# Early branches through later code, prefetch hints at its end, and another first load, in a decode kernel fed by DMA

## Chip, cores, metric

One core of a Trainium2 chip. The metric is device time in microseconds (us) of one execution. All executions told of here were in the normal (fast) state.

## The reference

One decode step: layer norm of x, attention of 32 query heads over a cache of 65,536 positions in 4 key-value heads, and beside it a mixer MLP on the same normalized x. Both are added to x.

```python
# cut to what matters; shapes: D 1024, Hq 32, Hkv 4, Sk 65536, Dh 128, F 3584; bfloat16
xn  = layernorm(x)                                        # x: [1, 1, 1024]
q   = xn @ wq                                             # wq: [1024, 4096]
p   = softmax(q . k_cache * Dh**-0.5)                     # k_cache: [1, 4, 65536, 128]
a   = (p . v_cache) @ wo                                  # wo: [4096, 1024]
h   = gelu(layernorm(xn) @ w1)                            # w1, w2: [1024, 1024]
x1  = xn + shift(h) @ w2                                  # one token: the shifts leave zeros
b   = x1 + gelu(layernorm(x1) @ w3) @ w4                  # w3: [1024, 3584], w4: [3584, 1024]
out = x + a + b
```

170 MB are read, nearly all of it the cache, for one token.

## The kernel before

The parts that the change and the argument touch. Each engine's instructions are recorded in a queue (`q_pe`, `q_dve`, ...) and emitted at the end. All large loads go through SyncE's DMA queue (`q_sp`) into three slots of 8.4 MB; x goes through ScalarE's.

```python
        _dma(q_act, chan("x"), lambda e: e.dma_start(out=x_bf, in_=...), writes=[b_x])
        kv_load(0, "s0", rows_src(A_wq, 0, 8), 8 * HQD)          # 8.4 MB, 65,536 bytes a partition
        b_w1 = b_KV[1][0:2]
        b_w2 = b_KV[1][2:4]
        kv_load(1, "w1", rows_src(B_w1, 0, 8), 8 * D, b_w1)      # 2.1 MB, 16,384 bytes a partition
        _dma(q_sp, chan("w2"), ...)
        kv_load(2, "s2", rows_src(B_w3, 0, 8), 8 * F)
# ... cut: constants on POOL, layer norm, q projection, MLP; then for each of 8 blocks of the cache:
            Ttr(n)          # VectorE transposes K in place
            QK(n)           # TensorE: scores
            # ... cut: MAX, EXP, PT, PTr, PV, FLUSH
            issue(6 + 2 * m)                                     # V of the next block
            issue(7 + 2 * m)                                     # K of the one after
# ... cut; at the end w4 comes in four parts, each followed by its matmuls, then the output:
        for i, (r0, nr) in enumerate(w4_parts):                  # rows 17, 7, 3, 1
            out_rows([...], [b_W4[i], b_gh], last=(i == len(w4_parts) - 1))
        _op(q_dve, lambda e: e.tensor_copy(orow[:, :], OUT), reads=[b_OUT], writes=[b_orow])
        ev_out = _dma(q_sp, chan("out"), lambda e: e.dma_start(out=..., in_=orow[0:97:32, :]), reads=[b_orow])
        q_sp.wait_all([ev_out])
# emission: one straight program an engine; only TensorE has a loop, over the 4 heads
        for eng in (nc.sync.engine, nc.scalar.engine):           # one DMA of each goes ahead of the opening barrier
            first = next(i for i in code[n_before:] if i.engine == eng)
            code.remove(first)
            code.insert(code.index(heads[eng]), first)
        q_pool.emit(nc.gpsimd)
        q_dve.emit(nc.vector)
# ... cut
        q_pe.emit(nc.tensor, q_pe.ops[:marks[0]])
        with nc.tensor.Fori(0, HKV):
            # ... cut
        q_pe.emit(nc.tensor, q_pe.ops[marks[-1]:])
```

## Time and profile before

| | before |
|---|---|
| time | 400.48 us median of 3 runs (400.39 to 400.56) |
| span of the profile | 399.1 us |
| data moved | 169.87 MB, 426 GB/s |
| TensorE, VectorE busy | 42%, 55% |
| first matmul, q projection starts | 6.63, 27.53 us |
| last part of w4 landed: first engine, last engine | 394.45, 396.56 us |
| from there to the end of the span | 2.52 us |

The kernel keeps the 16 DMA engines full from the first microsecond to the last. Lines of the page of the kernel before: the DMA row (busy share in tenths in 40 slices of 10 us), and the queues (packets, MB, share of 16 engines' span). q1 is SyncE's data queue, q10 ScalarE's, and the two of kind "instruction" carry the engines' own code. In all lines of the profile PE is TensorE's matmuls, PEld its weight loads, DVE VectorE, ACT ScalarE, POOL GpSimd, SPq SyncE's queue, and L379 a line of the kernel; "engine" alone, in the text on packets, is one of the 16 DMA engines.

```profile
span 399.1 us, 3429 instructions
PE 168.9 (42%) x1523; PEld 59.0 (15%) x1484; DVE 221.4 (55%) x260; ACT 23.9 (6%) x50; POOL 7.7 (2%) x31
...
DMA  9999899999999999999999999999999999999995
...
q1 hardware_dynamic: 3608, 169.87, 98.7%
q8 instruction: 5, 0.08, 0.1%
q10 hardware_dynamic: 144, 0.00, 0.0%
q14 instruction: 2, 0.02, 0.0%
```

So the time is a sum of three: when the DMA engine that is done first has delivered its share of the last load, how much later the slowest engine is, and what follows. The compute is hidden. The next lines are from the chain that ended last (start, length, what): long DMA waits with short computations between them, and at the end a wait for w4, four matmuls and one copy.

```profile
0.12 22.10 DMA KV<-in_A_x_dram
...
27.53 5.03 PE S_ps L379 x64
...
138.97 46.66 DMA KV<-in_A_k_cache_dram
...
363.64 32.91 DMA KV<-in_B_w_dram
396.60 0.31 PE S_ps L566 x4
396.94 0.42 DVE orow L647
```

And from the waits of SyncE's queue (who waited for what: us, times, longest): the final wait, for the output to land.

```profile
SPq L73 <- DMA out_dram<-orow: 1.0, 1, 1.0
SPq L728 <- PEq L728: 0.3, 1, 0.3
```

The second line is the opening barrier.

The trace also records single packets. The table gives the instruction packets of the kernel before that ran within its span (start in us, duration, bytes, queue). Those on q8 are TensorE's; those on q14 are taken for VectorE's:

```
46.00  1.09 us  16384   q8        52.71  0.33 us  8192   q14
81.76  1.03     16384   q8       259.38  0.33     8192   q14
122.72 1.02     16384   q8
378.24 1.07     16384   q8
394.28 1.08     16384   q8
```

A 16,384-byte one and the data packet behind it, which takes 2.97 instead of 2.42 us, cost one engine about 1.6 us; a VectorE one 0.33 us and 0.66 us for its neighbour (3.08 us). The split of the data over the engines is static, as far as the trace shows: what an engine lost it did not make up. With the packets of each engine chained end to start, the engine that carried the fetch of 81.76 us was 1.72 us behind the first engine at 204 us and 1.71 us behind at 389 us. No packet of TensorE came between 122.72 and 378.24 us, while its loop ran three whole passes; the one in 147 to 225 us is 274 matmuls and 278 weight loads.

### The profile page before, as it was taken

The numbers are of one execution on the slowest core, as the hardware profiler recorded it, in microseconds if no ns is written. First come the engines' busy times: TensorE is split into PE (matmuls) and PEld (weight loads), VectorE is DVE, ScalarE is ACT, GpSimd is POOL, SyncE is SP. The second block draws the span as 40 slices with busy tenths as digits, with TensorE's granted clock in tenths as the row PEclk, the third lists the DMA queues.
The fourth block names the chain that finished last, engine by engine and source line by source line (L and its number), as shares of the span: only waits on it lengthen the run. The fifth ranks groups of instructions, "written<-read, shape, count | busy, mean of one in ns | idle before, by whom it ended". The sixth has DMA issues, their size and how long they took to land.

```text
span 399.1 us, 3429 instructions
## 1 busy us (share of the span) xinstructions
PE 168.9 (42%) x1523; PEld 59.0 (15%) x1484; DVE 221.4 (55%) x260; ACT 23.9 (6%) x50; POOL 7.7 (2%) x31
## 2 busy tenths in 40 slices
PE   0034767338033713460357036413541362137394
PEld 0011334012001210110012001101120110012232
DVE  0024222994298549833984597269647952895201
ACT  1000000011001100110011002000100110011000
POOL 5000000000000000000000000000000000000000
PEclk9998568555655665575557555855585558555969
DMA  9999899999999999999999999999999999999995
GB/s 420 420 388 493 383 441 466 447 415 427 420 427 429 434 460 434 434 427 420 434 427 420 466 440 434 421 420 434 427 427 466 434 440 420 420 427 434 418 414 229
DMA packets 3759, 169.97 MB, mean 426 GB/s; under 512 B 548, under 2 KB 552, under 8 KB 808
## 3 DMA queue, kind: packets, MB, share of 16 engines
q1 hardware_dynamic: 3608, 169.87, 98.7%
q8 instruction: 5, 0.08, 0.1%
q10 hardware_dynamic: 144, 0.00, 0.0%
q14 instruction: 2, 0.02, 0.0%
HBM read 169.87 MB, written 0.00 MB: 426 GB/s over the span
## 4 chain that ended last, share of the span: by engine, by line
DMA 59%; DVE 25%; PE 12%; issue 1%; ACT 1%; SPq 1%; POOL 0%
DMA KV<-in_A_k_cache_dram 45%; DVE KV L460 18%; DMA KV<-in_B_w_dram 8%; DMA KV<-in_A_x_dram 6%; PE S_ps L411 3%; PE OT_ps L518 2%; DVE mrow L481 2%; PE M_ps L426 2%; PE S_ps L474 2%; PE S_ps L379 1%; ACT p_sb L496 1%; DVE Yall L395 1%; DVE pT_f L509 1%; DVE pT_f L419 1%; PE PT_ps L505 0%
## 5 line engine op out<-in xcount | busy, mean ns | idle before, releaser
L460 DVE STREAM_TRANSPOSE KV<-KV 128x4096 f32<-128x4096 f32 x32 | 140.3, 4422 | 44.3 <-DMA KV<-in_A_k_cache_dram 44.3
L474 PE MATMUL S_ps<-KV,Ycur 128*32 128x512 bf16 x512 | 60.7, 624 | 132.5 <-DVE KV L460 132.5
L518 PE MATMUL OT_ps<-KV,pT_f 128*32 128x512 bf16 x512 | 47.2, 511 | 4.0 <-issue 3.0
L474 PEld LDWEIGHTS S_ps<-KV,Ycur 128*32 128x32 bf16 x512 | 14.3, 126 | 160.0 <-DVE KV L460 142.4
L496 ACT ACTIVATE p_sb<-S_ps,brun 128x1024 bf16<-128x1024 f32 x16 | 17.8, 1114 | 276.6 <-DVE brun L494 176.1
L509 DVE STREAM_TRANSPOSE pT_f<-PT_ps 128x512 f32<-128x512 f32 x32 | 22.5, 702 | 14.0 <-PE PT_ps L505 14.0
L481 DVE TENSOR_REDUCE mrow<-S_ps 128x1 f32<-128x1024 f32 x16 | 19.3, 1205 | 11.3 <-PE S_ps L474 11.3
L484 PE MATMUL M_ps<-Rm,Lmat 128*128 128x16 bf16 x16 | 3.1, 194 | 38.0 <-DVE Rm L482 38.0
L529 DVE SCALAR_TENSOR_TENSOR O_acc<-O_acc,ff,OT_ps 128x512 f32<-128x512 f32 x12 | 9.0, 748 | 14.7 <-PE OT_ps L518 14.7
L518 PEld LDWEIGHTS OT_ps<-KV,pT_f 128*32 128x32 bf16 x512 | 13.1, 115 | 23.8 <-issue 16.4
L411 PE MATMUL S_ps<-KV 128*32 128x512 bf16 x88 | 12.1, 538 | 2.7 <-DVE KV L359 2.7
L339 DVE CAST KV<-KV 128x8 f32<-128x8 bf16 x1 | 0.2, 172 | 22.2 <-DMA KV<-in_A_x_dram 22.2
L578 PE MATMUL S_ps<-KV,o_bf 128*1 128x512 bf16 x64 | 9.9, 484 | 4.5 <-DMA KV<-in_A_wo_dram 4.5
L505 PE MATMUL PT_ps<-p_sb,permR 128*128 128x512 bf16 x16 | 9.7, 607 | 0.8
L426 PE MATMUL M_ps<-ident_f,pT_f 64*128 64x2 f32 (+2 forms) x32 | 7.9, 373 | 2.5 <-DVE pT_f L419 2.5
L484 PEld LDWEIGHTS M_ps<-Rm,Lmat 128*128 128x128 bf16 x16 | 1.7, 104 | 49.3 <-DVE Rm L482 49.3
L582 DVE COPY pT_f<-S_ps 1x512 f32<-1x512 f32 x1 | 0.7, 679 | 14.4 <-PE S_ps L578 14.4
L426 PEld LDWEIGHTS M_ps<-ident_f,pT_f 64*128 64x128 f32 (+2 forms) x32 | 7.7, 326 | 4.7 <-DVE pT_f L419 3.1
L419 DVE COPY pT_f<-S_ps 64x512 f32<-64x512 f32 (+1 forms) x3 | 2.1, 685 | 10.8 <-PE S_ps L411 10.8
L505 PEld LDWEIGHTS PT_ps<-p_sb,permR 128*128 128x128 bf16 x32 | 3.3, 102 | 27.5 <-ACT p_sb L496 14.7
L364 PE MATMUL M_ps<-KV 8*128 8x8 bf16 x1 | 0.2, 184 | 16.1 <-DVE Dmat_f L363 16.1
L642 POOL MEMSET pT_f<- 64x512 f32 x1 | 0.5, 520 | 312.4 <-PE OT_ps L518 312.4
(88 smaller groups left out, 90.2 us busy)
## 6 DMA issues: line engine op xcount, KB each, us to landing
KV<-in_B_w_dram SPq DMA_DIRECT2D x1, 7168.0 KB, 48.0
KV<-in_B_w_dram SPq DMA_DIRECT2D x1, 4352.0 KB, 27.4
KV<-in_B_w_dram SPq DMA_DIRECT2D x2, 2048.0 KB, 28.3
KV<-in_B_w_dram SPq DMA_DIRECT2D x1, 1792.0 KB, 31.3
KV<-in_B_w_dram SPq DMA_DIRECT2D x1, 768.0 KB, 32.7
KV<-in_B_w_dram SPq DMA_DIRECT2D x1, 256.0 KB, 32.9
KV<-in_A_k_cache_dram SPq DMA_DIRECT2D x8, 46.7
KV<-in_A_v_cache_dram SPq DMA_DIRECT2D x8, 28.1
```

What stands on the lines that cost most here:

```text
L411: fns.append(lambda e, j=j, k=k, mv=mv: e.matmul(S_ps[32 * (k % 4):32 * (k % 4) + 32, bank + k // 4, :], vec[:, j:j + 1].broadcast_to([P, ...
L419: _op(q_dve, lambda e, b=b, nb=nb: e.tensor_copy(pT_f[0:32 * nb, b, :], S_ps[0:32 * nb, bank + b, :]), reads=[b_S[bank + b]], writes=[b_pT ...
L426: fns.append(lambda e, b=b, nb=nb, c=c: e.matmul(M_ps[:, c0 + 16 * b + c:c0 + 16 * b + 4 * nb:4], pT_f[0:32 * nb, b, c:512:4], ident_f[0:3 ...
L460: _op(q_dve, lambda e: e.transpose(out=KV32[:, s, o:o + 4096], in_=KV32[:, s, o:o + 4096]), reads=[b_KV[s][sub]], writes=[b_KV[s][sub]], l ...
L474: fns.append(lambda e, we=we, cm=cm, mv=mv: e.matmul(S_ps[32 * cm:32 * cm + 32, n % 4, :], Ycur[:, we, :, :].rearrange("p a g -> p (a g)") ...
L481: _op(q_dve, lambda e: e.reduce_max(mrow[:, k:k + 1], S_ps[:, 2 * k:2 * k + 2, :].rearrange("p b c -> p (b c)"), axis=AX.X), reads=b_S[2 * ...
L496: _op(q_act, lambda e: e.activation(p_sb[:, :, :].rearrange("p b c -> p (b c)"), S_ps[:, 2 * k:2 * k + 2, :].rearrange("p b c -> p (b c)") ...
L505: _op(q_pe, lambda e: e.matmul(PT_ps[:, :], permR[:, :], p_sb[:, n % 2, :], start=True, stop=True), reads=[b_p[n % 2], b_const], writes=[b ...
L509: _op(q_dve, lambda e: e.transpose(out=pT_f[:, n % 2, :], in_=PT_ps[:, :]), reads=[b_PT], writes=[b_pT[n % 2]], loop=True)
L518: fns.append(lambda e, q=q, q4=q4: e.matmul(OT_ps[32 * q4:32 * q4 + 32, g % 2, :], pT_bf[:, n % 2, q, :, 1], KV[:, s, 8192 * sub + 512 * q ...
L529: _op(q_dve, lambda e: e.scalar_tensor_tensor(out=O_acc[:, 0:512], in0=O_acc[:, 0:512], scalar=ff[:, k:k + 1], in1=OT_ps[:, k, :], op0=ALU ...
L578: _grp(q_pe, [lambda e, j=j, jj=jj: e.matmul(S_ps[32 * jj:32 * jj + 1, 1, :], o_bf[:, j:j + 1], KV[:, 0, j * D + 512 * jj:j * D + 512 * (j ...
```

## The change

Its intent: fetch code early instead of among the data. TensorE and VectorE jump through small stubs that lie further on in their code, so that instruction packets come at the start. The last part of the code of each has a hint (BRANCH_PREFETCH_HINT in the trace) that names a stub; it is meant to keep the packets of 259.38 and 394.28 us out of the data. w1 goes first because its packets are small (16,384 bytes in 0.61 us, against 65,536 in 2.42 for wq), so that early fetches and x, which share the engines with it, wait less. SyncE issues four loads ahead of the opening barrier instead of one.

```diff
@@ loads
-        kv_load(0, "s0", rows_src(A_wq, 0, 8), 8 * HQD)
         kv_load(1, "w1", rows_src(B_w1, 0, 8), 8 * D, b_w1)
+        kv_load(0, "s0", rows_src(A_wq, 0, 8), 8 * HQD)
@@ emission (cut)
-        for eng in (nc.sync.engine, nc.scalar.engine):
+        for eng, n_early in ((nc.sync.engine, 4), (nc.scalar.engine, 1)):
@@
-        q_dve.emit(nc.vector)
+        def visit(e, stub, nxt, back, within=None):
+            go(e, back)                       # branch over the stub
+            label(stub)
+            nc.engines[e].nop(nofuse=True)
+            go(e, nxt)                        # the early path goes on from here
+            label(back, within)
+
+        go(dve, "dve_v1")                     # first thing that VectorE does
+        label("dve_open")
+        open_barrier(dve)
+        q_dve.emit(nc.vector, q_dve.ops[:dve_cut])
+        visit(dve, "dve_v1", "dve_open", "dve_a")
+        go(dve, "dve_b")
+        label("dve_last")
+        nc.vector.nop(nofuse=True)
+        go(dve, "dve_end")
+        label("dve_b")
+        dve_hint = nc.vector.mark_branch_hint_location()
+        q_dve.emit(nc.vector, q_dve.ops[dve_cut:])
+        nc.vector.br("dve_last").branch_hint(dve_hint)
+        label("dve_end")
@@ TensorE (cut): stubs v1 and v2 ahead of the barrier, v3 and v4 after it, v2 and v3 inside the loop's body
+        go(pe, "pe_v1")
+        label("pe_open")
+        open_barrier(pe)
+        go(pe, "pe_v3")
+        label("pe_a")
...
+        label("pe_f")
+        pe_hint = nc.tensor.mark_branch_hint_location()
+        q_pe.emit(nc.tensor, q_pe.ops[pe_cut3:])
+        nc.tensor.br("pe_last").branch_hint(pe_hint)
+        label("pe_end")
```

The last branch of each engine goes back to a stub, and from there on to the end of the program.

More of the change, by code (lines that the diff above doesn't have):

```diff
@@ L447, in bass_parallel_sum__gqa_block_cached__mixer_s_mlp__decode_kernel @@
         layer_norm(x1, b_x1, xn3, xn3_bf, b_xn3, 208)
+        pe_cut0 = len(q_pe.ops)
         proj(2, 0, F, xn3_bf, 0, b_KV[2] + [b_xn3], 288)
@@ L639, in bass_parallel_sum__gqa_block_cached__mixer_s_mlp__decode_kernel @@
                 combine(h)
+            if m == 1:
+                dve_cut = len(q_dve.ops)
         loop_sync(HKV)
@@ L644, in bass_parallel_sum__gqa_block_cached__mixer_s_mlp__decode_kernel @@
         wo_rows()
+        pe_cut3 = len(q_pe.ops)
         for i, (r0, nr) in enumerate(w4_parts):
@@ L651, in bass_parallel_sum__gqa_block_cached__mixer_s_mlp__decode_kernel @@
         code = nc.m.functions[0].blocks[0].instructions
-        heads = {e: next(i for i in code if i.opcode == "Drain" and i.engine == e) for e in (nc.sync.engine, nc.scalar.engine)}
+        pe, dve = nc.tensor.engine, nc.vector.engine
+        opening = {e: [i for i in code if i.engine == e and i.opcode in ("Drain", "EventSemaphore")] for e in (pe, dve, nc.sync.engine, nc.scalar.engine)}
         n_before = len(code)
@@ L655, in bass_parallel_sum__gqa_block_cached__mixer_s_mlp__decode_kernel, with go, label, open_barrier @@
         q_act.emit(nc.scalar)
-        for eng in (nc.sync.engine, nc.scalar.engine):
-            first = next(i for i in code[n_before:] if i.engine == eng)
-            assert first.opcode == "DMACopy" and not first.sync_info.on_wait
-            code.remove(first)
-            code.insert(code.index(heads[eng]), first)
-        q_pool.emit(nc.gpsimd)
-        q_dve.emit(nc.vector)
+        for eng, n_early in ((nc.sync.engine, 4), (nc.scalar.engine, 1)):
+            for first in [i for i in code[n_before:] if i.engine == eng][:n_early]:
+                assert first.opcode == "DMACopy" and not first.sync_info.on_wait
+                code.remove(first)
+                code.insert(code.index(opening[eng][0]), first)
+        q_pool.emit(nc.gpsimd)
+        def go(e, name):
+            nc.br(name, engines=[e])
+        def label(name, within=None):
+            nc.switch_bb(name, parent=within)
+        def open_barrier(e):
+            here = nc.m.functions[0].blocks[-1].instructions
+            for i in opening[e]:
+                code.remove(i)
+                here.append(i)
+        def visit(e, stub, nxt, back, within=None):
[18 more added lines that the diff above has]
+        label("dve_end")
         marks = [i for i, o in enumerate(q_pe.ops) if o[0] == 3]
@@ L690, in bass_parallel_sum__gqa_block_cached__mixer_s_mlp__decode_kernel @@
             assert [(o[0], o[2]) for o in body] == [(o[0], o[2]) for o in work[0]]
-        q_pe.emit(nc.tensor, q_pe.ops[:marks[0]])
+        nc.tensor.nop(nofuse=True)
+        go(pe, "pe_v1")
+        label("pe_open")
+        n_pe = len(nc.m.functions[0].blocks) - 1
+        open_barrier(pe)
+        go(pe, "pe_v3")
+        label("pe_a")
+        q_pe.emit(nc.tensor, q_pe.ops[:pe_cut0])
+        visit(pe, "pe_v1", "pe_v2", "pe_b")
+        q_pe.emit(nc.tensor, q_pe.ops[pe_cut0:marks[0]])
         for s_, v in entry.items():
@@ L694, in bass_parallel_sum__gqa_block_cached__mixer_s_mlp__decode_kernel @@
         with nc.tensor.Fori(0, HKV):
-            for waits, o in zip(steps, work[0]):
+            body_bb = nc.bb_map[nc.m.functions[0].blocks[-1].name]
+            for k, (waits, o) in enumerate(zip(steps, work[0])):
+                if k == 100:
+                    visit(pe, "pe_v2", "pe_open", "pe_c", body_bb)
+                if k == 220:
+                    visit(pe, "pe_v3", "pe_v4", "pe_d", body_bb)
                 for s_, v in waits.items():
@@ L700, in bass_parallel_sum__gqa_block_cached__mixer_s_mlp__decode_kernel @@
                 nc.tensor.wait_ge(s_, v).then_inc(s_, -v)
-        q_pe.emit(nc.tensor, q_pe.ops[marks[-1]:])
+        q_pe.emit(nc.tensor, q_pe.ops[marks[-1]:pe_cut3])
+        visit(pe, "pe_v4", "pe_a", "pe_e")
+        go(pe, "pe_f")
+        label("pe_last")
+        nc.tensor.nop(nofuse=True)
+        go(pe, "pe_end")
+        label("pe_f")
[3 more added lines that the diff above has]
+        label("pe_end")
         prev, n_ld = None, 0
+        code = next(b for b in nc.m.functions[0].blocks if b.name == "pe_a").instructions
         for k, i in enumerate(code):
@@ L713, in bass_parallel_sum__gqa_block_cached__mixer_s_mlp__decode_kernel @@
             prev = key
-        assert n_ld > 40, n_ld
+        assert n_ld > 20, n_ld
 _INS = ['A_x', 'A_k_cache', 'A_v_cache', 'A_wq', 'A_wo', 'B_x', 'B_w1', 'B_w2', 'B_w3', 'B_w4']
```

## The prediction

> **What bounds the kernel.** The page has VectorE busy 55% and TensorE 42%; its queue part gives the data queue 98.7% of 16 engines' span: 169.87 MB, mean 426 GB/s. In the packet records a 65,536-byte packet takes 2.42 us, 27.07 bytes/ns an engine. An engine's 10.62 MB need 392.2 us; the first packet starts 1.0 us into the span, the first round of packets takes about 3.1 instead of 2.42 us, and what follows the last landing (396.56) takes 2.5 us. The table of DMA issues shows K loads waiting 46.7 us from issue to landing, although 8.39 MB at this rate take 19.4: queued work hides compute.
>
> **Where 2 us are left.** The packet records also hold instruction packets, placed among the data: five of 16,384 bytes (TensorE, at 46.0, 81.8, 122.7, 378.2, 394.3 us) and two of 8,192 (VectorE, 52.7 and 259.4). Each sits on one engine. A 16 KB one takes 1.03-1.09 us and the data packet beside it about 0.55 us more: 1.6 us. An 8 KB one takes 0.33 us and its neighbour 0.66 more: 1.0 us. Data are divided statically, so an engine never makes this up. Chaining packets end to start shows ten engines that finish at 394.0-394.6, five at about 395.4-396.0, and the one with both VectorE packets last, at 396.1. The final load therefore lands at 396.56, its first engine at 394.45: 2.1 us of skew, which is the whole prize.
>
> [...]
>
> **What the change does.** Branches through stubs pull TensorE's and VectorE's later blocks at the start[...]. w1 ahead of wq puts 16 KB packets (0.61 us) beside the early fetches and lets x, whose 16-byte packets alternate with the load in front, land near 6 us, not 22.2. [...] wq and w1 together still land near 26.9; the q projection starts near 27.3 (27.5 before). The first layer norm (5.3 us) fits long before that. Branches in the loop cost well under 1 us and are hidden.
>
> **On the critical path.** Only the slowest engine. Two fetches vanish, the rest move early but still occupy engines, save what runs before the first data packet at 1.0 us. No engine should carry two, so the slowest has +0.6 to +1.6 instead of +2.0: gain 0.4 to 1.4 us, at most 2.0. Prediction **399.5 us**, 8 in 10 between **398.3 and 400.6**; faster by over 2%: 0.01, within 2%: 0.98, slower by over 2%: 0.01.
>
> **Marks of each step.** Right: no 16,384-byte instruction packet after about 20 us; x lands at 5-8 us; w4's last landing 395-396.2, skew between its first and last engine 0.8-1.7 us; loop spacing (77.5 us for two blocks) and the tail of 2.5 us unchanged; DMA share 99%.
>
> **What would make it wrong.** Early fetches falling on one engine, adding up to more than 2 us;[...] the barrier so late that the q projection and with it the first K load slip past the queued 20 MB (beyond 47 us); a tail block missing at the end, a visible stall before the last matmuls; or early fetches that cost nothing, giving 398.4.

The sum: the slowest engine at +0.6 to +1.6 us instead of +2.0, so 0.4 to 1.4 us off 400.48, put at 399.5. But its "two fetches" that vanish (TensorE's of 394.3 us and VectorE's of 259.4) were then expectation only. Where the text has no figure, the traces have: a branch of TensorE's loop takes 0.08 to 0.23 us in the kernel before and 0.08 to 0.22 in the changed one, and x's 128 packets of 16 bytes come 16 to a round of data packets, each within 0.03 us of the end of one (both kernels). That a branch can stall is shown by the changed kernel (5.57 to 7.09 us).

## The result, and the profile after

| | before | changed |
|---|---|---|
| time | 400.44 us (400.37 to 400.56, 4 runs) | 400.87 us (400.77 to 401.15, 4 runs) |
| first matmul, q projection starts | 6.63, 27.53 us | 21.41, 28.49 us |
| x landed, wq landed | 22.21, 22.02 us | 11.32, 28.35 us |
| w4 landed: first engine, last engine | 394.45, 396.56 us | 394.52, 396.40 us |
| from there to the end | 2.52 us | 3.35 us |
| span | 399.1 us | 399.8 us |

The ratio is 1.0012 (95% interval 0.9994 to 1.0029). A ratio is the mean time of one kernel's fast runs over that of the other's of the same rounds, so it is not quite the ratio of the medians quoted here. The time lies above the predicted 398.3 to 400.6.

Lines of the page of the changed kernel:

```profile
span 399.8 us, 3478 instructions
PE 167.6 (42%) x1523; PEld 59.8 (15%) x1508; DVE 221.5 (55%) x260; ACT 23.9 (6%) x50; POOL 7.6 (2%) x31
...
DMA  9999999999999999999999999999999999999994
...
q1 hardware_dynamic: 3608, 169.87, 98.6%
q8 instruction: 5, 0.08, 0.1%
q10 hardware_dynamic: 144, 0.00, 0.0%
q14 instruction: 3, 0.02, 0.0%
```

The number of TensorE's instruction packets has not fallen, and q14 has one more. (24 weight loads more come from a last pass over the code that now sees only the first block; they are hidden.) The chain that ended last:

```profile
0.45 27.91 DMA KV<-in_A_wq_dram
28.49 4.97 PE S_ps L379 x64
...
138.97 46.67 DMA KV<-in_A_k_cache_dram
...
363.48 32.92 DMA KV<-in_B_w_dram
```

Its beginning is a microsecond later, yet the K load is awaited from the same 138.97 us on, and w4 lands 0.16 us earlier. And the two waits of SyncE's queue:

```profile
SPq L791 <- PEq L791: 4.4, 1, 4.4
SPq L73 <- DMA out_dram<-orow: 1.8, 1, 1.8
```

The barrier holds SyncE for 4.4 us, until TensorE is there, as intended. The wait for the output went from 1.0 to 1.8 us, which was not. That is the loss in the span of the profiled run: -0.16 us for the landing of w4, +0.10 from there to the issue of the output (0.83 to 0.93), +0.73 from the issue to the end (1.69 to 2.42), together +0.7 (399.1 to 399.8). This run was the slowest of the four (401.15 us); the spans of the other three were 399.5 and 399.6, so that the usual loss is nearer to the 0.4 us of the medians.

The packets say why (changed kernel, start in us, duration, bytes):

```
  3.92  0.96 us  16384   q8         4.09  0.31 us   8192   q14
 11.60  0.89     16384   q8       392.82  0.31      8192   q14
 18.73  0.90     16384   q8       398.18  0.55      8192   q14
 26.26  1.01     16384   q8
397.73  1.06     16384   q8
output, 512 bytes on each of 4 engines: 398.56  398.58  398.59  398.73
its completions reach SyncE at:         398.98  398.99  399.00  399.73
```

One quarter of the output starts where the packet of 398.18 ends, and its completion is 0.73 us behind the third. In the kernel before, the four completions are 0.06 us apart. The late quarter starts only 0.14 us after the third, so most of the 0.73 us lies between its packet and its completion; the trace does not show what happens there. Ahead of the packets the trace has the branches: TensorE's last two at 396.45 and 396.71 us, VectorE's at 396.90 and 397.17. Each packet follows the start of the second of its engine's two by 1.0 us.

### The profile page after: what moved, and what is told of

Its sections match the earlier page's. It is cut to its first block, busy times and chain, and to the rows that moved or that the text cites. A ratio compares the mean times of both kernels' runs of the same rounds, so it can differ in the third digit from the quotient of the medians.

```text
span 399.8 us, 3478 instructions
## 1 busy us (share of the span) xinstructions
PE 167.6 (42%) x1523; PEld 59.8 (15%) x1508; DVE 221.5 (55%) x260; ACT 23.9 (6%) x50; POOL 7.6 (2%) x31
## 4 chain that ended last, share of the span: by engine, by line
DMA 60%; DVE 25%; PE 12%; issue 1%; ACT 1%; SPq 1%; POOL 0%
DMA KV<-in_A_k_cache_dram 45%; DVE KV L461 17%; DMA KV<-in_B_w_dram 8%; DMA KV<-in_A_wq_dram 7%; PE S_ps L411 3%; PE OT_ps L519 2%; DVE mrow L482 2%; PE M_ps L426 2%; PE S_ps L475 2%; PE S_ps L379 1%; ACT p_sb L497 1%; DVE Yall L395 1%; DVE pT_f L510 1%; DVE pT_f L419 1%; PE PT_ps L506 0%
## 5 line engine op out<-in xcount | busy, mean ns | idle before, releaser
L482 DVE TENSOR_REDUCE mrow<-S_ps 128x1 f32<-128x1024 f32 x16 | 19.3, 1205 | 11.3 <-PE S_ps L475 11.3
L579 PE MATMUL S_ps<-KV,o_bf 128*1 128x512 bf16 x64 | 8.7, 439 | 4.5 <-DMA KV<-in_A_wo_dram 4.5
L361 PE MATMUL M_ps<-KV 8*128 8x128 bf16 x1 | 0.3, 284 | 21.4 <-issue 21.4
L339 DVE CAST KV<-KV 128x8 f32<-128x8 bf16 x1 | 0.2, 223 | 11.3 <-DMA KV<-in_A_x_dram 11.3
```

Of the source, the lines that this page charges most:

```text
L482: _op(q_dve, lambda e: e.reduce_max(mrow[:, k:k + 1], S_ps[:, 2 * k:2 * k + 2, :].rearrange("p b c -> p (b c)"), axis=AX.X), reads=b_S[2 * ...
L579: _grp(q_pe, [lambda e, j=j, jj=jj: e.matmul(S_ps[32 * jj:32 * jj + 1, 1, :], o_bf[:, j:j + 1], KV[:, 0, j * D + 512 * jj:j * D + 512 * (j ...
```

## The experiments

Theory 1: the early fetches gain 0.2 us, and the last branches release fetches that lose more at the output. Theory 2: the late start of TensorE costs the time. Theory 3, which came up on the way: w1 first costs something itself. In 12 kernels with 5 runs each, all correct, the span is again written as first engine done + lag of the last engine + tail; this sum can be read from each trace to 0.05 us. "Output" is the distance between the first and last of its completions.

| kernel | w4, first engine | lag | tail | output | time, median (range) |
|---|---|---|---|---|---|
| before | 394.45 | 2.11 | 2.52 | 0.06 | 400.44 |
| changed | 394.52 | 1.88 | 3.35 | 0.74 | 400.87 (400.77-401.15) |
| no_end_jumps | 394.69 | 2.17 | 2.62 | 0.06 | 400.72 (400.61-400.78) |
| no_dve_end_jump | 394.69 | 2.20 | 2.52 | 0.06 | 400.65 (400.52-400.79) |
| no_pe_end_jump | 394.60 | 1.84 | 3.17 | 0.54 | 401.05 (400.81-401.36) |
| w1_first_only | 394.76 | 2.18 | 2.52 | 0.06 | 400.70 (400.44-400.78) |
| wq_first_visits | 394.37 | 1.85 | 3.16 | 0.64 | 400.93 (400.63-401.11) |
| wq_visits_late_jump | 394.40 | 2.03 | 2.82 | 0.06 | 401.12 (401.01-401.31) |
| hints_late_jump | 394.56 | 2.02 | 2.82 | 0.05 | 401.21 (401.16-401.28) |
| before_again | 394.53 | 2.21 | 2.52 | 0.07 | 400.50 (400.38-400.81) |
| late_start | 396.48 | 2.06 | 2.52 | 0.06 | 403.21 (402.41-403.95) |
| hints_only | 394.46 | 1.86 | 3.37 | 0.77 | 400.94 (400.79-401.19) |
| wq_visits_early_jump | 394.44 | 1.80 | 2.52 | 0.06 | 400.26 (400.08-400.32) |
| hints_early_jump | 394.54 | 1.92 | 2.53 | 0.07 | 400.24 (400.19-400.38) |

The kernel before, timed beside each batch, had medians of 400.41 to 400.44 us, within 400.26 to 400.77.

### no_end_jumps, no_dve_end_jump, no_pe_end_jump: the last branches taken away

```diff
 # no_dve_end_jump: VectorE's hint and last branch
-        dve_hint = nc.vector.mark_branch_hint_location()
         q_dve.emit(nc.vector, q_dve.ops[dve_cut:])
-        nc.vector.br("dve_last").branch_hint(dve_hint)
 # no_pe_end_jump: the same two lines of TensorE; no_end_jumps: both
-        pe_hint = nc.tensor.mark_branch_hint_location()
         q_pe.emit(nc.tensor, q_pe.ops[pe_cut3:])
-        nc.tensor.br("pe_last").branch_hint(pe_hint)
```

> The changed kernel without both hints and without the branches back to the last stubs; the early branches and w1 first stay. Theory 1 (the loss is at the end: instruction packets released by the last branches hold back one engine's share of the output): no instruction packet after 396 us, the output's four completions within 0.1 us of each other again (0.74 us apart in the changed kernel, 0.06 before), tail from the last w4 landing to the end 2.5 us instead of 3.3; a VectorE fetch returns in the loop near 255 us, a TensorE one near 393. Time 400.2 to 400.5, 0.4 to 0.6 below the changed kernel. Theory 2 (the late opening barrier and TensorE's first matmul at 21.4 us cost the time): time stays at 400.9, as the start is the same.

> The changed kernel without VectorE's hint and last branch; TensorE keeps its own. Theory 1 in its form A (VectorE's 8,192-byte packet at 398.18 us is the one that holds back the output): output completions together, time 400.2 to 400.5, although a VectorE fetch returns in the loop on the engine that has the early one (0.85 + 1.0 us on it). Form B (TensorE's 16,384-byte packet at 397.73 us does it): output still 0.7 us apart, 400.8 to 401. Theory 2: 400.9.

> The changed kernel without TensorE's hint and last branch; VectorE keeps its own. Form A: output still 0.7 us apart, 400.8 to 401. Form B: output together, 400.2 to 400.4. A TensorE fetch returns near 393 us in both, on an engine of its own. Theory 2: 400.9.

Measured: with VectorE's last branch gone the output is together (0.06 us) and the tail is 2.52 or 2.62 us; with only TensorE's gone it is not (0.54 us, tail 3.17; 1.0016 of the kernel before, interval 1.0002 to 1.0030). The same wait of SyncE's queue, first in no_dve_end_jump, then in no_pe_end_jump:

```profile
SPq L73 <- DMA out_dram<-orow: 1.0, 1, 1.0
```

```profile
SPq L73 <- DMA out_dram<-orow: 1.6, 1, 1.6
```

So it is VectorE's packet, form A. TensorE's 16,384-byte packet is still there in no_dve_end_jump, at 398.22 us, and does the output no harm in that run. But the time did not fall to the 400.2 to 400.5 that I had written down. Without its hint a VectorE packet is in the loop again (at 259.68 and 259.71 us) on the engine that already carries its early packet, and the lag is back at 2.2 us: in this kernel the hint hangs on the branch, and each way costs about as much as it saves. A remainder of 0.2 us is in the first column, where all three stand at 394.60 or more against 394.45. That led to theory 3.

### w1_first_only: the order of the loads alone

```diff
 # on the kernel before
-        kv_load(0, "s0", rows_src(A_wq, 0, 8), 8 * HQD)
         kv_load(1, "w1", rows_src(B_w1, 0, 8), 8 * D, b_w1)
+        kv_load(0, "s0", rows_src(A_wq, 0, 8), 8 * HQD)
```

> The kernel before with w1 ahead of wq, nothing else. Both theories: no change in time (400.3 to 400.6), since the two loads together are the same bytes; x lands at 7 to 10 us instead of 22.2, wq at 26.9 to 27.1, and the q projection starts within 0.5 us of 27.5. If this alone moves the time by more than 0.2 us, the order of loads and not the fetches explains part of the result.

Measured: x landed at 10.26 us, wq at 27.21, the q projection started at 27.35, and the span has its first engine done at 394.76, the latest of all but late_start; 400.70 us, with a range that overlaps that of the kernel before. By the medians (0.26 us) the mark of 0.2 us is just passed, by the ratio (1.0004, 0.16 us) it is not; one kernel cannot settle 0.2 us.

### wq_first_visits, wq_visits_late_jump, hints_late_jump, before_again

```diff
 # wq_first_visits: the changed kernel with the two loads in their old order
+        kv_load(0, "s0", rows_src(A_wq, 0, 8), 8 * HQD)
         kv_load(1, "w1", rows_src(B_w1, 0, 8), 8 * D, b_w1)
-        kv_load(0, "s0", rows_src(A_wq, 0, 8), 8 * HQD)
 # wq_visits_late_jump: this, and VectorE's last branch held until the output has landed
         q_dve.emit(nc.vector, q_dve.ops[dve_cut:])
+        nc.vector.wait_ge(*ev_out)
         nc.vector.br("dve_last").branch_hint(dve_hint)
 # hints_late_jump: wq_visits_late_jump without early branches, and one early load of SyncE as before
         def visit(e, stub, nxt, back, within=None):
-            go(e, back)
-            label(stub)
-            nc.engines[e].nop(nofuse=True)
-            go(e, nxt)
-            label(back, within)
-
-        go(dve, "dve_v1")
-        label("dve_open")
-        open_barrier(dve)
+            pass
 # ... TensorE's early branches likewise. before_again: a comment
```

> The changed kernel with wq ahead of w1 again; early branches, hints and last branches stay. What the first four runs leave: the four kernels with w1 first have their earliest DMA engine done with the last w4 part at 394.5 to 394.8 us, the kernel before at 394.45. Theory 3 (w1 first costs all engines 0.1 to 0.3 us at the start): earliest engine 394.4 to 394.5, slowest 1.6 us later by the early TensorE packets, output again 0.5 to 0.7 us late on one engine; time 400.3 to 400.7. If the order costs nothing: 400.8 to 401.1. Each early TensorE branch takes at least the 7.1 us it takes beside 65,536-byte packets in the changed kernel, so its first matmul comes at 25 us or later and the q projection up to some us after 27.5, which theory 2 would pay for and theory 1 not.

> The same with VectorE's last branch held until the output has landed. Theory 1: output completions within 0.1 us, no VectorE fetch before the output's packets, slowest engine 1.6 us behind the earliest against 2.1 in the kernel before; 0.4 to 0.7 us below the kernel with wq first and early branches, 399.9 to 400.2, so a little faster than the kernel before. If the end of VectorE's program then ends the execution later, 0.2 to 0.4 of it is lost again.

> The kernel before with only the two hints and last branches, VectorE's held until the output has landed; no early branches, wq first. If the gain is that two fetches no longer fall into the data (and not that the others come early): VectorE fetch near 53 us but none near 259, TensorE fetches near 46, 82, 123 and 378 but none near 394; slowest engine 1.6 us behind the earliest; time 399.9 to 400.2, as with the early branches. If early fetching is worth something itself: 400.3 or more.

> The kernel before with a comment added, for a second profile of it and the noise of the comparison. Time 400.3 to 400.6, ratio 1.000 within 0.0007, earliest engine at 394.4 to 394.5, slowest 2.1 us later. If the earliest engine comes at 394.7 here, the shift of the kernels with w1 first is noise.

Measured. wq_first_visits has its first engine done at 394.37 us, but took 400.93: not theory 3's 400.3 to 400.7. TensorE's first matmul did not come later either (21.27 us, expected 25 or more), as its branches beside the large packets took what they took in the changed kernel. before_again agrees with the kernel before (ratio 1.0004), and its first engine is at 394.53. Over all traces the five kernels with w1 first have 394.52 to 394.76, mean 394.65, and the eight with wq first (without late_start) 394.37 to 394.56, mean 394.47. So w1 first costs about 0.2 us in the traces; in the times, 400.87 against 400.93 for otherwise equal kernels, it doesn't show.

The two kernels that hold VectorE's branch missed clearly. The output was together, spans were 399.25 and 399.40, but the times were 401.12 and 401.21, the slowest of all but late_start. In the profiled runs the time exceeds the span by 1.76 and 1.88 us, against 1.25 in the kernel before: in wq_visits_late_jump VectorE now branches at 398.93 and 399.20 us and has a packet from 400.22 to 400.75, and the time of this run is 401.01; that the execution has to wait for this packet is likely, but not shown. This was foreseen as a loss of 0.2 to 0.4 us and was 0.5 to 0.6. Holding the fetch back is no better than letting it meet the output.

### late_start: the late start by itself

```diff
 # on the kernel before
+        for _ in range(12):
+            ev = q_pool.op(lambda e: e.memset(KV[:, 1, 16 * D:20 * D].bitcast(F32), 0.0))
+            q_pool.wait_all([ev])
         evs = []
```

> The kernel before with 12 useless memsets ahead of the POOL constants, nothing else: POOL ready some 20 us later, TensorE's first matmul at about 27 us (6.6 before, 21.4 in the changed kernel), q projection at about 33 (27.5 and 28.5), first K load issued about 6 us later. Theory 2 (the late start costs time): 405 to 407, or at least the 0.4 us of the changed kernel in proportion, 402 and more. Theory 1: the queued loads hide it, 400.3 to 400.6, K landings within 0.3 us of those before.

Measured: 403.21 us, 2.8 more than the kernel before (ratio 1.0077, 1.0063 to 1.0090). Theory 1's text was wrong; of theory 2's the 405 to 407 was wrong, and only its weaker form, 402 and more, held. A start late by 7 us (q projection at 34.48) does cost time, though less than its length. The reason is in the loop's first block. SyncE issues V of the second block when the first block is computed, and the queue runs dry if that comes too late. SyncE's issues in order of time, of the kernel before, the changed kernel and late_start:

```profile
99.84 0.33 SPq L290 DMA_DIRECT2D KV<-in_A_v_cache_dram  x1
100.21 0.43 SPq L290 DMA_DIRECT2D KV<-in_A_k_cache_dram  x1
```

```profile
100.67 0.33 SPq L290 DMA_DIRECT2D KV<-in_A_v_cache_dram  x1
101.04 0.43 SPq L290 DMA_DIRECT2D KV<-in_A_k_cache_dram  x1
```

```profile
106.32 0.33 SPq L290 DMA_DIRECT2D KV<-in_A_v_cache_dram  x1
106.69 0.43 SPq L290 DMA_DIRECT2D KV<-in_A_k_cache_dram  x1
```

The load ahead of them in the queue, K of the second block, landed at 108.19, 108.20 and 107.99 us. The issue thus came 8.4, 7.5 and 1.7 us ahead of the end of the queued work, and only the last lead was too short: this V landed at 127.56, 127.56 and 129.08 us. In the packet records of late_start no packet of data starts between 105.13 and 107.28 us, where in the kernel before one load follows the other without a gap. The 1.5 us stayed to the end, where the first engine was done 2.0 us later. The profiled run was the fastest of the five (402.41 us); what the others lost beyond 2.0 us was not profiled. The changed kernel, 0.8 us later here, is on the safe side. Theory 2 is right as a mechanism and wrong for this change. My own statement that the queue hides everything up to 47 us looked at the wrong load.

### hints_only, wq_visits_early_jump, hints_early_jump: the fault alone, and the mended kernel

```diff
 # hints_only: the kernel before with both hints and last branches, without early branches
 # wq_visits_early_jump, on wq_first_visits; hints_early_jump, the same on hints_only
-        q_dve.emit(nc.vector, q_dve.ops[dve_cut:])
+        dve_out = len(q_dve.ops) - 1
+        while q_dve.ops[dve_out - 1][0] == 0:
+            dve_out -= 1
+        q_dve.emit(nc.vector, q_dve.ops[dve_cut:dve_out])
+        nc.vector.wait_ge(chans["w42"].sem, 16)       # the third part of w4 has landed
         nc.vector.br("dve_last").branch_hint(dve_hint)
         label("dve_end")
+        q_dve.emit(nc.vector, q_dve.ops[dve_out:])    # the copy that the output waits for
```

> The kernel before with the two hints and the immediate last branches, without early branches, wq first. It has the suspected fault by itself: no VectorE packet near 259 us but one near 398, output's last completion 0.5 to 0.8 us behind the others, tail 3.1 to 3.3 us; slowest engine 1.8 to 2.1 us behind the earliest; time 400.6 to 401.0. If the output is together here, the fault needs the early branches.

> wq first, early branches and hints, with VectorE's last branch moved ahead of its last copy: it waits for the third part of w4 (395.6 us), branches, and then copies. Its instruction packet then runs near 397.2 to 397.8 us, after its engine's data and before the output's packets at 398.5. Theory 1: output completions within 0.1 us, tail 2.5 us, earliest engine 394.4, slowest 1.9 to 2.0 later: span 398.8 to 398.9, time 400.0 to 400.2, 0.2 to 0.4 below the kernel before. If the packet still meets the output, or VectorE stalls on the branch, 400.6 or more.

> The same end without early branches: the kernel before, hints, VectorE's last branch ahead of its last copy. If early fetching is worth nothing by itself: 400.0 to 400.3, within 0.15 us of the kernel with early branches. TensorE fetches near 46, 82, 121 and 377 us, VectorE at 53 and 397; slowest engine 1.9 to 2.0 us behind the earliest.

Measured: hints_only has the fault without any early branch (VectorE packet at 398.13 us, output 0.77 us apart, tail 3.37, 400.94 us). With VectorE's branch 1.3 us earlier its packet runs at 396.92 us for 0.43 us in wq_visits_early_jump (397.14 and 0.54 in hints_early_jump), after the data and before the output, and again 1.0 us behind the branch. The wait of SyncE's queue in wq_visits_early_jump:

```profile
SPq L73 <- DMA out_dram<-orow: 1.0, 1, 1.0
```

The tail is 2.52 us and the times are 400.26 and 400.24, as low for the kernel without early branches as for the one with them: early fetching by itself is worth nothing that these runs could measure. The clearest pair is hints_only and hints_early_jump, timed in the same rounds and different only in where VectorE branches: 400.94 us (400.79 to 401.19) against 400.24 (400.19 to 400.38). Both kernels with the early jump are 0.2 us below the kernel before timed beside them (400.44); the ten runs of the two lie within 400.08 to 400.38, the nine of the kernel before within 400.30 to 400.64. The intervals of the ratios, 0.9980 to 1.0008 and 0.9981 to 1.0008, still hold 1; by the sum in the traces it is a gain of 0.1 to 0.3 us in the span.

## Why the prediction was wrong

- **Right: what bounds the kernel.** The data queue took 98.4% to 98.8% of the engines' span in all kernels, and no variant but late_start moved the time by more than 0.8 us. That the whole lag of about 2 us is a prize is not shown: it was 1.80 to 2.21 us in every kernel.
- **Right: an instruction packet cost its engine time that it did not make up.** Removing the hint brought the packet near 259 us back, and the lag with it: 1.88 to 2.20 us.
- **The step that failed: "Two fetches vanish, the rest move early".** They did not vanish. The packets near 259 and 394 us went, but each engine had another one 1.0 us behind its last branch: TensorE's at 397.73 and VectorE's at 398.18 us. (VectorE's comes 1.01 to 1.06 us behind the start of its last branch in all eight kernels that have one, wherever the branch is put.) With both hints the changed kernel has no packet where the kernel before has those of 259.38 and 394.28 us, and without VectorE's hint its packet is there again (259.68 us in no_dve_end_jump); but the branch that carries the hint leads to the end of the program at last, and 1.0 us behind it there is a packet after all. (Whether it carries the same code is not shown, as the packet records hold no addresses.) VectorE's meets the output. With it falls the mark "the tail of 2.5 us unchanged": it was 3.35. no_dve_end_jump (2.52), hints_only (3.37) and the kernels with the branch moved (2.52, 2.53) show this cause from three sides. With the packet out of the output's way, the last two took 400.26 and 400.24 us, within the range foretold. The mark "no 16,384-byte instruction packet after about 20 us" failed too: there was one at 26.26 and one at 397.73 us.
- **Mis-sized: the gain, 0.4 to 1.4 us.** The lag fell by 0.23 us, from 2.11 to 1.88, and the last landing by 0.16. An early TensorE packet costs 0.96 us and 0.47 for the 16,384-byte data packet behind it (1.08 instead of 0.61), 1.43 in all, as expected; but engines start at different times, and the one that carried the packet of 3.92 us also began late (its first data packet at 1.32 us against 1.01, found by chaining packets end to start). The last engine was 1.9 us behind the first when w1 landed (7.02 and 8.89 us), and it stayed so for 388 us. The engines that carried no fetch at all lie up to 0.63 us apart (387.22 to 387.85 at the end of the first part of w4, chained). I had taken the lag for the fetch alone. The fetch at 26.26 us left its engine almost as late (389.04, the last one 389.12): early or not, a fetch among the data costs its engine about the same.
- **Mis-sized without harm: the early branches.** The barrier came 5.9 us later (POOL's first memset behind it at 6.79 instead of 0.91 us), and POOL's constants were ready at 12.44; the estimate had both too early. What the prediction left out are the two stubs that TensorE visits behind the barrier: its first matmul, which had waited for the constants, now came at 21.4 us. Line of the order in time, before and changed:

```profile
6.63 0.28 PE L361 MATMUL M_ps<-KV 8*128 8x128 bf16 x1 [6.63 <-POOL KV L322]
```

```profile
21.41 0.28 PE L361 MATMUL M_ps<-KV 8*128 8x128 bf16 x1 [21.41 <-issue]
```

  The trace has the branches: 0.31 us to the first stub, 5.57 to the second, then 7.09 and 7.09. In each of the three long ones a 16,384-byte packet starts (3.92, 11.60, 18.73 us), and the branch ends 1.4 to 1.5 us after the end of this packet (at 6.25, 13.97, 21.11 us). The other taken branches of TensorE took 163 to 312 ns in the changed kernel, those of VectorE 41 to 58. x landed at 11.3 us, not 5 to 8. Its 16-byte packets, on a queue of their own, landed with the 8.4 MB beside it in the kernel before (22.21 and 22.02 us). With the packets of each engine chained, x's eight packets follow the data one by one in both kernels. In the changed kernel x's come to lie one packet behind those of w1, so that the completion of x has to let the first 65,536-byte packet of wq pass: x landed 2.43 us after w1 (8.89 and 11.32), as long as that packet takes. The prediction had missed this one packet.
- **Right in the conclusion, wrong in the reason: the late start is hidden.** The lead that counts is 8.4 us, at the first V load of the loop; late_start used it up. (The V loads of later blocks have leads as short, 8.2 to 9.1 us, but kept 7.9 to 9.8 in late_start.)

What stays open: whether w1 first costs 0.2 us in time as it does in the traces; whose code the 8,192-byte packet near 393 us is (all nine kernels with a hint have it, at 392.7 to 394.0 us, and none of the others); and how VectorE's packet holds back a completion by 0.5 to 0.8 us when the quarter of the output starts only 0.1 to 0.3 us late, and why on one of four engines, that is, whether it would always be the same one.

## What to carry to other kernels

In these kernels static loads fill all DMA engines (98.4% to 98.8% of their span), the slowest engine sets the end (396.56 us, the first one at 394.45), and what a code fetch cost an engine stayed with it (1.72 us at 204 us, 1.71 at 389). But moving a fetch paid only where no engine was awaited, between the last data and the output (400.26 and 400.24 us against 400.44). With a small output on its way it cost 0.6 to 0.9 us of the tail, and with the fetch behind the output the time exceeded the span by 0.5 to 0.6 us more. After a change of control flow, list where every instruction packet went, at the end of the program above all, before counting any as removed. And when something is said to be hidden by queued work, find the load with the shortest lead that the delay can reach, not the first one.
